# An attention kernel with expert routing, rewritten around rows: wider exponentials, token rows scattered by slot, all expert work at the end

## The chip, the cores and the metric

The kernel runs on one core of a Trainium2 chip. The metric is device time in microseconds (us) of that core, lower is better. Every job also ran the kernel before on the same chip. Results of different jobs are compared by their ratio to the kernel before of the same rounds, not by their microseconds.

## The reference, cut to what matters

```python
# q, k, v: 8 batches x 8 heads x 1152 x 64
q_pool = q.reshape(B, H, S // 2, 2, D).mean(axis=3)            # 576 queries a head
scores = scale * np.matmul(q_pool, k.transpose(0, 1, 3, 2))
attn = np.exp(scores - scores.max(-1, keepdims=True))
attn = attn / (attn.sum(-1, keepdims=True) + 1e-09)
x = (attn @ v)                                                 # -> 4608 tokens of 512
# 8 experts; each token goes to the one that domain_id names
for e in range(8):
    h = np.maximum(x[domain_id == e] @ w1[e], 0.0)             # 512 -> 1024
    out[domain_id == e] = h @ w2[e]                            # 1024 -> 512
```

The attention is done by pairs of heads, 32 pairs. AV below is the second product of attention, `attn @ v`. The traces show a matmul as two instructions, a load of one operand (PEld) and the matmul itself (PE); AV of the kernel before has 1152 of each. The operand that is loaded is called stationary here, the other moving. Both kernels give each expert 640 slots for rows, 40 tiles of 128 in all, whether filled or not.

## The kernel before

Attention: 576 steps. A step computes 128 keys by 288 queries for two heads, one exponential of 576 columns, and (three steps later) two AV matmuls with the values stationary. The result is transposed, features on partitions, so the softmax sums lie along one row and the reciprocals take a trip through DRAM to reach all partitions.

```python
def expo(t):                                   # 576 of these, 2 x 288 columns
    e_ = ering.tile([P, 2, QH], F16, name="e")
    et[t] = e_
    nc.scalar.activation(e_[:, :, :], st.pop(t)[:, :, 0:QH], AF.Exp, bias=0.0, scale=0.0625)

def norm_a(p):                                 # sums out of one row ...
    sr = work.tile([64, 18], FP32, name="srow")
    nc.sync.dma_start(sr[0:32, :], xu[p][0][64:65, :])
    nc.sync.dma_start(sr[32:64, :], xu[p][1][0:1, :])
    srec[p] = sr

def norm_b(p):                                 # ... reciprocal, to DRAM, back as a broadcast
    rr = work.tile([64, 18], FP32, name="rrow")
    nc.vector.reciprocal(rr[:, :], srec.pop(p)[:, :])
    nc.sync.dma_start(s_dram[p].rearrange("(a b) -> a b", a=64), rr[:, :])
    rb = work.tile([P, Sp], FP32, name="rb")
    for hh in range(2):
        nc.sync.dma_start(rb[64 * hh : 64 * hh + 64, :],
            s_dram[p, hh * Sp : (hh + 1) * Sp].unsqueeze(0).broadcast_to([64, Sp]))
    srec[p] = rb

def norm_c(p, hh):                             # ... multiply into xT, features x tokens
    nc.vector.tensor_tensor(out=xT[lo : lo + 64, 1 + b * Sp : 1 + (b + 1) * Sp, hp],
        in0=xu[p][hh][lo : lo + 64, :], in1=srec[p][lo : lo + 64, :], op=ALU.mult)

def gather(xs, j, e, t, hi, w=P):              # tokens of an expert, on POOL
    nc.gpsimd.indirect_copy(xs[:, j * P : (j + 1) * P, :], xT[:, 0:hi, :],
        idx[:, e, t * 8 : (t + 1) * 8], True)
# ... cut: two of an expert's five tiles are filler units inside the second half of attention;
# ... cut: the other three are the tail:
    for f in range(NF):
        for cc in range(ND):
            nc.tensor.matmul(hp_[:, 0:nsl], lhsT=w1h[:, cc, f * P : (f + 1) * P],
                rhs=xs[:, 0:nsl, cc],          # moving operand, element step 4
                start=cc == 0, stop=cc == ND - 1)
```

The softmax here doesn't subtract the row's maximum and nothing guards it: scores larger than these inputs give would overflow.

Of the kernel before, what the change touches and what calls it, by code (L numbers as in the profile page):

```python
# [19 lines left out]
def kernel(  # L20
# [16 lines left out]
    NT = N // P  # L37
# [4 lines left out]
    QH = Sp // 2  # L42
    QP = 96
    NJ = Sp // QP
    JH = NJ // 2
    R1 = 256
    R2 = 384
    CAP = R1 + R2
    NTC = CAP // P
    COLS = (N + R1) // 16  # L50
    EROW = 16 * COLS
    IC = CAP // 16
    I1 = NT // 2

    g_dram = nc.dram_tensor("g_slot", (E * EROW, 1), I32, kind="Internal").ap()
    s_dram = nc.dram_tensor("s_rec", (NPAIR, 2 * Sp), FP32, kind="Internal").ap()

    wpool = ctx.enter_context(tc.tile_pool(name="wpool", bufs=4))
    perm = ctx.enter_context(tc.tile_pool(name="perm", bufs=1))
    fbuf = ctx.enter_context(tc.tile_pool(name="fbuf", bufs=2))  # L60


    att = ExitStack()
    lds = att.enter_context(tc.tile_pool(name="lds", bufs=2))
    work = att.enter_context(tc.tile_pool(name="work", bufs=2))
    ering = att.enter_context(tc.tile_pool(name="ering", bufs=8))
    spsum = att.enter_context(tc.tile_pool(name="spsum", bufs=2, space=bass.MemoryType.PSUM))
    apsum = att.enter_context(tc.tile_pool(name="apsum", bufs=1, space=bass.MemoryType.PSUM))
    mpsum = att.enter_context(tc.tile_pool(name="mpsum", bufs=2, space=bass.MemoryType.PSUM))
# [6 lines left out]
    v16 = [perm.tile([P, NC, 2 * P], F16, name=f"v16_{i}") for i in range(NV)]  # L76
    ident = perm.tile([P, P], FP32, name="ident")
    ident16 = perm.tile([P, P], F16, name="ident16")
    xT = perm.tile([P, N + 1, HP], F16, name="xT")
# [3 lines left out]
    def pair_load(p):  # L83
        b, h = p // HP, 2 * (p % HP)
        q2 = lds.tile([QP, 2, NJ, 2 * D], FP32, name="q2")
        for hh in range(2):
            nc.sync.dma_start(
                q2[:, hh, :, :],
                q[b, h + hh].rearrange("(j p r) d -> p j (r d)", p=QP, j=NJ),
            )  # L90
        k16 = lds.tile([P, 2, NC, D], F16, name="k16")
        nc.gpsimd.dma_start(  # L92
            k16[:, :, :, :], k[b, h : h + 2].rearrange("h (p c) d -> p h c d", p=P)
        )
        vs = lds.tile([P, 2, NC, D], F16, name="vs")
        nc.gpsimd.dma_start(  # L96
            vs[:, :, :, :], v[b, h : h + 2].rearrange("h (p c) d -> p h c d", p=P)
        )
        loaded[p] = {"q2": q2, "k16": k16, "vs": vs}

    pair_load(0)
    pair_load(1)


    make_identity(nc, ident[:, :])
    nc.vector.tensor_copy(ident16[:, :], ident[:, :])
    for i in range(NV):
        nc.vector.memset(v16[i][:, :, D : D + P], 1.0)
# [11 lines left out]
    n_iota = perm.tile([P, NT], I32, name="n_iota")  # L120
    nc.gpsimd.iota(n_iota[:, :], pattern=[[P, NT]], base=0, channel_multiplier=1)
    dom = perm.tile([NT, 2 * P], I32, name="dom")
    nc.sync.dma_start(dom[:, :], moe_domain_id.bitcast(I32).rearrange("(i q) -> i q", i=NT))
    g_init = perm.tile([P, E * EROW // P], I32, name="g_init")
    nc.gpsimd.memset(g_init[:, :], N)
    nc.sync.dma_start(g_dram.rearrange("(a b) one -> a (b one)", a=P), g_init[:, :])
    nc.gpsimd.memset(xT[:, 0:1, :], 0.0)
# [4 lines left out]
    def rt_a():  # L132
        d16 = perm.tile([NT, P], F16, name="d16")
        nc.vector.tensor_copy(d16[:, :], dom[:, 0 : 2 * P : 2])
# [6 lines left out]
        mt = mpsum.tile([P, 1024], F16, name="mt")  # L141
        nc.tensor.transpose(mt[:, 0:NT], in_=d16[:, :], identity=ident16[0:NT, 0:NT])
        dall = perm.tile([P, NT], FP32, name="dall")
        nc.vector.tensor_copy(dall[:, :], mt[:, 0:NT])
# [9 lines left out]
    PADC = 32  # L154

    def rt_b():
# [5 lines left out]
        mc = mpsum.tile([P, 512], FP32, name="mt")  # L162
# [4 lines left out]
        mr = mpsum.tile([P, 512], FP32, name="mt")  # L167
# [13 lines left out]
    def rt_c():  # L181
        inc = rt["sc"][0]
        oh, cum, dall = rt["oh"], rt["cum"], rt["dall"]
        delta = perm.tile([P, E], FP32, name="delta")
        nc.vector.tensor_scalar(
            out=delta[:, :], in0=inc[:, :, PADC + I1 - 1], scalar1=-1.0, scalar2=float(R1),
            op0=ALU.mult, op1=ALU.add,
        )
        nc.vector.tensor_scalar(
            out=delta[:, :], in0=delta[:, :], scalar1=0.0, scalar2=None, op0=ALU.max  # L190
        )
# [3 lines left out]
        nc.vector.tensor_tensor(  # L195
            out=cum[:, :, I1:], in0=cum[:, :, I1:],
            in1=delta[:, :].unsqueeze(2).broadcast_to([P, E, NT - I1]), op=ALU.add,
        )
# [4 lines left out]
        )  # L203
        ov = perm.tile([1, E], FP32, name="ov")
        nc.vector.tensor_tensor(
            out=ov[:, :], in0=inc[0:1, :, PADC + NT - 1], in1=delta[0:1, :], op=ALU.add
# [14 lines left out]
        si = perm.tile([P, NT], I32, name="si")  # L221
        nc.vector.tensor_copy(si[:, :], slot[:, :])
        sr = perm.tile([P, NT], I32, name="sr")
        nc.vector.tensor_single_scalar(out=sr[:, :], in_=si[:, :], scalar=15, op=ALU.bitwise_and)
        scol = perm.tile([P, NT], I32, name="scol")
        nc.vector.tensor_single_scalar(out=scol[:, :], in_=si[:, :], scalar=4, op=ALU.arith_shift_right)
        af = perm.tile([P, NT], FP32, name="af")
        nc.vector.scalar_tensor_tensor(
            out=af[:, :], in0=sr[:, :], scalar=float(COLS), in1=scol[:, :], op0=ALU.mult, op1=ALU.add
        )  # L230
        addr = perm.tile([P, NT], I32, name="addr")
        nc.vector.scalar_tensor_tensor(
            out=addr[:, :], in0=dall[:, :], scalar=float(EROW), in1=af[:, :], op0=ALU.mult, op1=ALU.add
        )
        rt.update(addr=addr, ovi=ovi)

    gap = perm.tile([1, 1], FP32, name="gap")

    def rt_scatter(i):
        nc.gpsimd.memset(gap[:, :], 0.0)  # L240
        ins = nc.gpsimd.indirect_dma_start(
            out=g_dram[:, :],
            out_offset=bass.IndirectOffsetOnAxis(ap=rt["addr"][:, i : i + 1], axis=0),
            in_=n_iota[:, i : i + 1],
            in_offset=None,
        )
        tc.declare_no_dep(ins.ins, group="gscat", reason="slots are unique")
        tc.add_to_no_dep_group("gscat", ins.ins)

    gidx = perm.tile([P, E, IC], I32, name="gidx")  # L250
    gtok = perm.tile([P, E, NTC], I32, name="gtok")
    idx = perm.tile([P, E, IC], U16, name="idx")
    gv = g_dram.rearrange("(e p c) one -> p e (c one)", e=E, p=16)

    def rt_read(a):
        nc.sync.dma_start(gidx[16 * a : 16 * a + 16, :, :], gv[:, :, 0:IC])

    def make_idx(dst, src, w):
        m1 = fbuf.tile([P, w], FP32, name=f"m1_{w}")
        nc.vector.tensor_scalar(  # L260
            out=m1[:, :], in0=src, scalar1=float(N), scalar2=4.0, op0=ALU.is_lt, op1=ALU.mult
        )
        m2 = fbuf.tile([P, w], FP32, name=f"m2_{w}")
        nc.vector.tensor_scalar(out=m2[:, :], in0=src, scalar1=1.0, scalar2=None, op0=ALU.add)
        nc.vector.tensor_tensor(out=dst, in0=m2[:, :], in1=m1[:, :], op=ALU.mult)

    own = perm.tile([P, 8], FP32, name="own")

    def rt_own():
        grp = perm.tile([P, 1], I32, name="grp")  # L270
        nc.vector.tensor_single_scalar(
            out=grp[:, :], in_=n_iota[:, 0:1], scalar=4, op=ALU.arith_shift_right
        )
        nc.vector.tensor_tensor(
            out=own[:, :], in0=iota_e[:, :], in1=grp[:, 0:1].broadcast_to([P, 8]), op=ALU.is_equal
        )

    def make_tok(dst, src, w):
        mk = fbuf.tile([P, w, 8], FP32, name=f"mk_{w}")
        nc.vector.tensor_tensor(  # L280
            out=mk[:, :, :], in0=src, in1=own[:, :].unsqueeze(1).broadcast_to([P, w, 8]), op=ALU.mult
        )
        mf = fbuf.tile([P, w], FP32, name=f"mf_{w}")
        nc.vector.tensor_reduce(mf[:, :], mk[:, :, :], mybir.AxisListType.X, ALU.add)
        nc.vector.tensor_copy(dst, mf[:, :])

    def rt_idx():
        rt_own()
        make_tok(
            gtok[:, :, :].rearrange("p e t -> p (e t)"),  # L290
            gidx[:, :, :].rearrange("p e (t a) -> p (e t) a", a=8),
            E * NTC,
        )
        make_idx(
            idx[:, :, :].rearrange("p e c -> p (e c)"),
            gidx[:, :, :].rearrange("p e c -> p (e c)"),
            E * IC,
        )
# [22 lines left out]
    def gather(xs, j, e, t, hi, w=P):  # L321
        nc.gpsimd.indirect_copy(  # L322
            xs[:, j * P : (j + 1) * P, :],
            xT[:, 0:hi, :],
            idx[:, e, t * 8 : (t + 1) * 8],
            True,
        )

    def scatter_out(osb, ap):
        nc.gpsimd.memset(gap[:, :], 0.0)  # L330
        ins = nc.gpsimd.indirect_dma_start(  # L331
            out=out[:, :],
            out_offset=bass.IndirectOffsetOnAxis(ap=ap, axis=0),
            in_=osb[:, :],
# [219 lines left out]
    for t in range(NST + 3):  # L554
# [49 lines left out]
        if t == 4:  # L604
            rt_b()
# [141 lines left out]
```

## Time and profile before

| | us |
|---|---|
| kernel before, median (742.57 to 746.84) | 745.72 |
| the profiled run's span | 771.9 |

The profiled execution took 773.81 us, 3.8% more than the median of the timed ones, although it is recorded as fast.

The engines are PE (matmuls; PEld is its loads of stationary operands), ACT (exponentials), DVE (other elementwise work), POOL (gathers, and the issue of many DMAs) and SP (issues DMAs only). "issue" as a releaser means that the profile shows nothing that the engine waited for. The first extract, of the kernel before, cuts the span into stretches (us from the start) and gives for each the busy time of each engine, the instructions in brackets, the granted TensorE clock and the DMA engines' share.

```profile
core 0: us, PE busy (x) PEld busy (x) DVE busy (x) ACT busy (x) POOL busy (x), PEclk, DMA share, GB/s
0.00:17.60 17.60, 2.47 (x20) 1.95 (x21) 8.50 (x22) 1.29 (x2) 6.19 (x18) 1.00 1.00 203
17.60:321.00 303.40, 216.72 (x1509) 144.04 (x1508) 158.66 (x309) 192.10 (x313) 76.46 (x124) 0.87 0.62 112
321.00:490.00 169.00, 164.29 (x1075) 103.89 (x1075) 104.75 (x206) 92.41 (x143) 56.50 (x78) 0.98 0.72 144
490.00:579.00 89.00, 78.24 (x571) 52.29 (x569) 55.44 (x99) 73.42 (x121) 7.22 (x9) 0.96 0.41 81
579.00:606.00 27.00, 0.07 (x2) 0.10 (x2) 4.59 (x6) 0.00 (x0) 2.60 (x3) 0.57 0.04 12
606.00:763.00 157.00, 129.53 (x448) 49.05 (x447) 23.36 (x40) 24.49 (x47) 55.11 (x83) 0.89 0.41 85
763.00:772.00 9.00, 0.07 (x1) 0.00 (x0) 0.00 (x0) 0.58 (x1) 1.42 (x3) 0.72 0.15 49
```

Row by row: start; attention alone; attention with expert filler; attention after the filler is used up; a dead stretch (PE 0.07 us in 27); the expert tail; the end. Attention alone keeps no engine busy: PE 217 of 303 us, ACT 192. The next extract is from the kernel before's list of waits (engine and line, what it waited for: total us, times, longest us).

```profile
ACT e L422 <- PE s L404: 189.9, 202, 15.6
...
DVE hT L656 <- PE hp L649: 124.4, 32, 18.2
...
PE mt L378 <- DVE kp L370: 64.0, 28, 10.0
...
DVE xT L471 <- DMA rb<-s_rec: 50.8, 19, 7.2
...
DVE rrow L458 <- DMA srow<-xuB: 45.3, 19, 6.0
```

ACT waits for scores, PE for DVE's copy of the keys (L378 transposes them), and DVE for the DMAs of the reciprocals' trip. DVE does its work in the order of the program here, so a wait for `rb` holds up the copies behind it: in this trace DVE is idle for 7.12 us until `rb` has landed, multiplies (131.22 to 134.12 us), copies the keys at 134.15, and PE, which waited 6.75 us for that copy, goes on at 135.01.

The groups of instructions of the kernel before (line, engine, operation, shapes, count, then busy us and mean ns of one, then idle time before them and what ended it):

```profile
L422 ACT ACTIVATE e<-s 128x576 f16<-128x576 f32 x576 | 357.9, 649 | 218.6 <-PE s L404 189.9 <-remote 17.5 <-PE accB L404 2.2
...
L649 PE MATMUL hp<-xs,w1h 128*128 128x384 f16 x256 | 88.3, 518 | 54.4 <-POOL gap L330 27.5 <-POOL xs L322 26.9
...
L662 PE MATMUL op<-w2h,hT 128*128 128x512 f16 x192 | 42.9, 380 | 0.0
...
L322 POOL INDIRECT_COPY xs<-xT,idx 128x512 f16 x40 | 35.8, 896 | 217.1 <-issue 187.6 <-PE s L404 25.2 <-PE hp L649 4.2
```

The gather (last line) looks cheap, 0.9 us of busy time, but the timeline of the kernel before around the first tail experts shows how far apart gathers are (start, duration, instruction, idle before it in brackets):

```profile
595.05 0.87 POOL L322 INDIRECT_COPY xs<-xT,idx 128x512 f16 x1 [53.05 <-issue]
600.07 0.87 POOL L322 INDIRECT_COPY xs<-xT,idx 128x512 f16 x1 [4.15 <-issue]
605.07 0.87 POOL L322 INDIRECT_COPY xs<-xT,idx 128x512 f16 x1 [4.13 <-issue]
605.99 11.04 PE L649 MATMUL hp<-xs,w1h 128*128 128x384 f16 x32 [26.93 <-POOL xs L322]
...
610.07 0.87 POOL L322 INDIRECT_COPY xs<-xT,idx 128x512 f16 x1 [4.13 <-issue]
...
616.85 5.36 PE L662 MATMUL op<-w2h,hT 128*128 128x512 f16 x24
```

The gathers start 5.0 us apart with 4.13 us of idle time for which the profile names no other cause. And 32 matmuls of 384 columns take 11.04 us, 340 ns each, where 24 of 512 columns with contiguous operands take 5.36, 216 each (216 x 23 + 380).

### The profile page before, as it was taken

To read this page: it belongs to the slowest core of one execution; us is meant where nothing else is said; L and a number is where in the kernel's file an instruction comes from. 1 tells how busy PE (TensorE), PEld (TensorE's weight loads), DVE (VectorE), ACT (ScalarE), POOL (GpSimd) and SP (SyncE) were. 2 spreads that over 40 slices of the span, in tenths; PEclk is the share of its full clock that TensorE was granted. 3 is DMA by queue.
4 is the path that set the end of the run, shared out by engine and by line. 5 is a ranking of instruction groups with operands and counts; after the bars stand their busy time and mean duration, and the time that the engine had idled before them with its cause. 6 is when DMAs were issued, how large, how long until landed. Compare 5 with 4: busy or idle time off the path is not lost.

```text
span 771.9 us, 10270 instructions
## 1 busy us (share of the span) xinstructions
PE 591.4 (77%) x3619; PEld 351.3 (46%) x3619; DVE 355.3 (46%) x680; ACT 384.3 (50%) x625; POOL 205.5 (27%) x316
## 2 busy tenths in 40 slices
PE   2857675948676887599999999888990597776885
PEld 1534443636454564366666666555660232222332
DVE  4744443545553765366666655665852111111111
ACT  1746564848575686355555555777890111111111
POOL 3264640211120100124343331210000144443331
PEclk9977978989899898799999999999995698988998
DMA  9344459785859445157999935654310065556001
GB/s 192 65 79 77 78 90 173 138 147 109 158 116 200 93 88 117 23 106 144 188 196 187 206 89 117 115 101 86 70 33 17 0 135 114 116 116 126 36 33 37
DMA packets 91006, 83.24 MB, mean 108 GB/s; under 512 B 12698, under 2 KB 78398, under 8 KB 90944
## 3 DMA queue, kind: packets, MB, share of 16 engines
q0 software_dynamic: 40960, 53.51, 39.6%
q1 hardware_dynamic: 49984, 28.98, 15.8%
q8 instruction: 30, 0.49, 0.3%
q14 instruction: 32, 0.26, 0.1%
HBM read 116.59 MB, written 10.81 MB: 165 GB/s over the span
## 4 chain that ended last, share of the span: by engine, by line
issue 22%; PE 20%; DVE 13%; DMA 12%; POOL 6%; POOLq 0%; SPq 0%; DVEq 0%
PE mt L404 9%; DVE xT L471 7%; DMA rb<-s_rec 4%; PE s L404 4%; DMA srow<-xuB 4%; POOL xs L322 3%; DMA s_rec<-rrow 3%; DVE kp L370 2%; PE accA L404 2%; PE accB L404 2%; POOL out_dram L331 2%; PE hp L649 2%; PE mt L378 1%; DVE v L359 1%; DMA srow<-xuA 1%
## 5 line engine op out<-in xcount | busy, mean ns | idle before, releaser
L422 ACT ACTIVATE e<-s 128x576 f16<-128x576 f32 x576 | 357.9, 649 | 218.6 <-PE s L404 189.9
L404 PE MATMUL s<-qz,kq 128*128 128x288 f16 x1152 | 250.5, 301 | 24.1 <-ACT e L422 12.4
L404 PE MATMUL accA<-e,v 128*128 128x288 f16 x576 | 169.9, 299 | 11.0 <-DVE xuA L445 7.9
L404 PE MATMUL accB<-e,v 128*128 128x288 f16 x576 | 169.4, 299 | 0.7 <-DVE xuB L445 0.3
L404 PEld LDWEIGHTS <-kq 128*128 128x128 f16 x1152 | 116.2, 103 | 110.8 <-issue 55.2
L404 PEld LDWEIGHTS <-v 128*128 128x128 f16 x1152 | 116.9, 101 | 49.4 <-issue 13.1
L649 PE MATMUL hp<-xs,w1h 128*128 128x384 f16 x256 | 88.3, 518 | 54.4 <-POOL gap L330 27.5
L322 POOL INDIRECT_COPY xs<-xT,idx 128x512 f16 x40 | 35.8, 896 | 217.1 <-issue 187.6
L649 PEld LDWEIGHTS <-w1h 128*128 128x128 f16 x256 | 30.1, 118 | 110.3 <-issue 107.5
L378 PE MATMUL mt<-ident,kp 128*128 128x128 f16 x256 | 23.2, 243 | 69.1 <-DVE kp L370 64.0
L656 DVE TENSOR_SCALAR hT<-hp 128x384 f16<-128x384 f32 x32 | 17.8, 557 | 124.4 <-PE hp L649 124.4
L404 PE MATMUL mt<-xs,w1h 128*128 128x256 f16 x256 | 68.6, 402 | 7.2 <-POOL xs L322 7.2
L96 POOL DMA_DIRECT2D vs<-in_v_dram x32 | 23.1, 722 | 189.9 <-DVE v L359 178.1
L654 ACT ACTIVATE hT<-hp 128x384 f16<-128x384 f32 x32 | 15.7, 491 | 116.3 <-PE hp L649 103.3
L471 DVE TENSOR_TENSOR xT<-xuA,rb 64x576 f16<-64x576 f32 x32 | 46.1, 1440 | 47.8 <-DMA rb<-s_rec 47.4
L331 POOL DMA_INDIRECT out_dram<-osb,gtok x40 | 44.8, 1119 | 57.5 <-DVE osb L512 41.6
L445 DVE COPY xuA<-accA 128x288 f32<-128x288 f32 x64 | 28.8, 450 | 62.9 <-PE accA L404 46.6
L378 PEld LDWEIGHTS <-kp 128*128 128x128 f16 x256 | 17.2, 109 | 79.5 <-DVE kp L370 73.9
L495 DVE TENSOR_SCALAR hT<-mt 128x256 f16<-128x256 f32 x64 | 27.1, 423 | 52.5 <-PE mt L404 52.5
L471 DVE TENSOR_TENSOR xT<-xuB,rb 64x576 f16<-64x576 f32 x32 | 46.3, 1448 | 4.4 <-DMA rb<-s_rec 3.5
L92 POOL DMA_DIRECT2D k<-in_k_dram x32 | 23.7, 742 | 85.4 <-DVE kp L370 80.4
L662 PE MATMUL op<-w2h,hT 128*128 128x512 f16 x192 | 42.9, 380 | 0.0
(83 smaller groups left out, 435.9 us busy)
## 6 DMA issues: line engine op xcount, KB each, us to landing
q<-in_q_dram SPq DMA_DIRECT2D x64, 288.0 KB
w1h<-in_moe_w_dram POOLq DMA_DIRECT2D x24, 512.0 KB
w2h<-in_moe_w_dram POOLq DMA_DIRECT2D x24, 512.0 KB
k<-in_k_dram POOLq DMA_DIRECT2D x32, 288.0 KB
vs<-in_v_dram POOLq DMA_DIRECT2D x32, 288.0 KB
rb<-s_rec SPq DMA_DIRECT2D x64, 144.0 KB
out_dram<-osb,gtok POOLq DMA_INDIRECT x40
g_slot<-n_iota,addr POOLq DMA_INDIRECT x36
```

Of the source, the lines that this page charges most:

```text
L92: nc.gpsimd.dma_start(k16[:, :, :, :], k[b, h : h + 2].rearrange("h (p c) d -> p h c d", p=P))
L96: nc.gpsimd.dma_start(vs[:, :, :, :], v[b, h : h + 2].rearrange("h (p c) d -> p h c d", p=P))
L322: nc.gpsimd.indirect_copy(xs[:, j * P : (j + 1) * P, :], xT[:, 0:hi, :], idx[:, e, t * 8 : (t + 1) * 8], True,)
L331: ins = nc.gpsimd.indirect_dma_start(out=out[:, :], out_offset=bass.IndirectOffsetOnAxis(ap=ap, axis=0), in_=osb[:, :], in_offset=None, bo ...
L378: nc.tensor.transpose(mt[:, c * P : (c + 1) * P], in_=k16[:, c, :, :].rearrange("p h d -> p (h d)"), identity=ident16[:, :])
L404: nc.tensor.matmul(out_, lhsT=lhsT, rhs=rhs, start=start, stop=stop)
L422: nc.scalar.activation(e_[:, :, :], st.pop(t)[:, :, 0:QH], AF.Exp, bias=0.0, scale=0.0625)
L445: nc.vector.tensor_copy(xu[p][head][:, hf * QH : (hf + 1) * QH], acc[u][head][:, 0:QH])
L471: nc.vector.tensor_tensor(out=xT[lo : lo + 64, 1 + b * Sp : 1 + (b + 1) * Sp, hp], in0=xu[p][hh][lo : lo + 64, :], in1=srec[p][lo : lo + 6 ...
L495: nc.vector.tensor_scalar(out=hts[e][:, f, :], in0=m[:, 0:R1], scalar1=0.0, scalar2=None, op0=ALU.max)
L649: nc.tensor.matmul(hp_[:, 0:nsl], lhsT=w1h[:, cc, f * P : (f + 1) * P], rhs=xs[:, 0:nsl, cc], start=cc == 0, stop=cc == ND - 1,)
L662: nc.tensor.matmul(op_[:, :], lhsT=hT[:, f, tt * P : (tt + 1) * P], rhs=w2h[:, f, :], start=f == 0, stop=f == NF - 1,)
```

## The change

The intent: take the waits out of attention, take the gathers out of the tail. The exponential becomes the stationary operand of AV (128 queries by 128 keys, with 64 values and a column of ones moving), so that a token is a row, its softmax sum lies beside it on the same partition, and DVE normalises with no DMA. Rows go by an indirect DMA to their slot in DRAM with the token's id as the last two elements; an expert's rows are read back contiguously and turned by PE. Keys are cast a pair ahead. The start changes too (the first pair's keys come uncast from SP, and 30 matmuls on zeros run first). The core of the diff, with cuts marked and some lines shortened:

```diff
-    QH = Sp // 2
+    W = 432
+    SPP = NC * Sp // W              # 12 steps a head pair, 384 in all
 ... cut
+    dom = perm.tile([P, B, NQ], I32, name="dom")
+    for i in range(NQ):             # nine DMAs of 4-byte elements
+        ... cut
+            nc.scalar.dma_start(dom[m : m + n, :, i : i + 1], dv_[pp : pp + n, :, j, 0:1])
 ... cut
-        e_ = ering.tile([P, 2, QH], F16, name="e")
-        nc.scalar.activation(e_[:, :, :], st.pop(t)[:, :, 0:QH], AF.Exp, ...)
+        if s_ % 4 == 0:
+            et[p, s_ // 4] = ering.tile([P, 2, 4 * W], F16, name="e")
+        nc.scalar.activation(e_[:, :, o : o + W], st.pop(t)[:, :, 0:W], AF.Exp, ...)
 ... cut
-        for head in range(2):
-            mm(acc[u][head][:, 0:QH], v16[p % NV][:, c, P * head : P * head + P], e_[:, head, :], ...)
+        for h in range(2):
+            for i in range(NQ):
+                nc.tensor.matmul(acc[p][h][:, i * (D + 1) : (i + 1) * (D + 1)],
+                    lhsT=e_[:, h, o + QO[i] : o + QO[i] + P],
+                    rhs=v16[p % NV][:, c, h, 0 : D + 1], ...)
 ... cut: norm_a, norm_b, norm_c and all gathers are removed
+            nc.vector.reciprocal(rr[:, :], a[:, :, D])
+            nc.vector.tensor_tensor(out=xb[b][:, :, hh * D : (hh + 1) * D], in0=a[:, :, 0:D],
+                in1=rr[:, :].unsqueeze(2).broadcast_to([P, NQ, D]), op=ALU.mult)
+    def put_x(b, i):
+        scatter(x_dram, xb[b][0:n, i, :], rt["addr"][0:n, ...], "xscat")
 ... cut: the filler units are removed
+    def turn(xs, n):                # rows -> features on partitions, contiguous
+        xt = tb.tile([P, ND, CAP], F16, name="xt")
+        ... four transposes a tile, copied out by DVE and ACT in turn
+    for e in range(3):
+        run(e, get_x(e, 0, NA), NA)                  # two tiles each
+    for e in range(E): ...          # then three tiles of experts 0 to 2, five of 3 to 7
```

## The prediction

> **What bounds the kernel now** (profiled span 771.9 us; unprofiled median 746.69). By the stretches view: start 17 us, attention alone 304 us, attention with expert filler 169 us, attention 90 us, a dead stretch of 26 us (PE busy 0.01 us), expert tail about 166 us.
> - Attention: the exponentials are 576 x 128x576. Back to back they start every 0.55 us, but in the undisturbed pattern every 0.65: two PSUM buffers make exp(t+1) wait for a score that waited for exp(t-1). Over 17-321 us a step costs 0.97 us (313 exps in 304 us). The list of waits: exponentials wait 190 us for scores; PE waits 64 us for DVE's key copy; DVE waits 51+45+12 us for the DMAs of the reciprocal round trip. With filler PE is 97% busy.
> - Tail: bound by POOL. The timeline shows one gather every 5.0 us (4.13 "issue" + 0.87); three gathers and the scatters make the 22 us period of an expert. PE needs only 16 us of it. There, 384-column matmuls go every 340 ns although 512-column ones with contiguous operands take 216: the moving operand has an element step of 4. [...]
>
> **What the change does**
> 1. 384 exponentials of 864. Duration 649 ns at 576 against 491 at 384 columns gives 0.82 ns per column: 0.89 us long, 0.78 us apart at best (301 us). With the two-buffer handshake (0.89 + about 0.76)/2 = 0.82 us a step.
> 2. AV: 2,880 matmuls of 65 columns instead of 1,152 of 288 (122 ns each, 141 us). The 96-column transposes with a weight load each go every 44 ns, so 44 is my ceiling, 30 my floor: 86-127 us. [...] the trace's 128-column transposes go every 57. PE per step: scores 0.37, AV 0.22-0.33, transposes 0.07, so 0.66-0.77 us: below ACT, barely.
> 3. The reciprocal round trip goes, DVE falls from 9.5 to about 5.6 us per head pair, keys are copied a pair ahead: those waits go. I take 0.87 us a step: 384 x 0.87 = 334 us, plus about 10 us of DMA stalls (5 MB slot-table fill early; weights in bursts).
> 4. Start: first exp at about 12.5 us instead of 17.6 (no PE wait for the domain ids).
> 5. Turn-over, PE idle: last evacuation, five serial scatters of 1.25 us, landing, row loads, first transposes: 14 us.
> 6. Experts all at the end, no gathers, contiguous operands: stage 1 69 us, stage 2 69 us, transposes with exposed evacuation about 24: 163 us.
> 7. End: 8 us as now.
> Sum 12.5 + 344 + 14 + 163 + 8 = 541 us profiled; the profile now is 3% over the timed run, so about 528 us.
>
> All on the critical path: attention goes from 563 to 344 us, the dead stretch from 26 to 14; the tail stays near 165 with all the experts in it.
>
> **Chances**: faster 0.98, same 0.01, slower 0.01; 8 in 10 within 495 to 575 us.
>
> **What would show it**: exponentials about 0.89 us each and 0.82-0.9 apart; AV matmuls 30-44 ns apart; no gathers; granted clock over 0.95; 512-column expert matmuls 216 ns apart; a PE gap of 10-16 us between the phases.
>
> **What would make it wrong**: AV pairs over 55 ns (PE-bound attention, +40 us); scattered rows or table fill clogging the queues so that q, k or v come late; weights late in the last experts; the clock dropping at pauses.

What is cut compared the trace with figures that no run here shows. Its floor of 30 ns for an AV matmul agrees with the trace's 44 ns at 96 columns taken in proportion to the columns, 29.8 at 65 (an estimate). Of a lower clock at a pause the trace of the kernel before has a case: 0.57 granted in the dead stretch, 0.96 in the stretch before it and 0.89 in the one after.

## The result, and the profile after

| kernel | median us | range | profiled span | granted clock |
|---|---|---|---|---|
| before | 745.72 | 742.57 to 746.84 | 771.9 | 0.902 |
| changed | 532.53 | 531.74 to 537.33 | 535.5 | 0.948 |

The ratio is 0.716 (95% interval 0.712 to 0.720). Ratios here are the mean time of one kernel's fast runs over that of the other's of the same rounds, so not quite the ratio of the medians.

The stretches of the changed kernel:

```profile
core 0: us, PE busy (x) PEld busy (x) DVE busy (x) ACT busy (x) POOL busy (x), PEclk, DMA share, GB/s
0.00:25.40 25.40, 8.29 (x51) 5.30 (x52) 7.04 (x21) 1.51 (x3) 7.62 (x22) 0.73 1.06 221
25.40:42.40 17.00, 7.14 (x59) 5.22 (x59) 5.63 (x17) 5.22 (x6) 0.90 (x2) 0.50 0.72 147
42.40:342.50 300.10, 288.76 (x4428) 227.54 (x4426) 157.06 (x389) 296.84 (x378) 98.15 (x153) 0.99 0.82 168
342.50:357.80 15.30, 1.48 (x17) 1.20 (x18) 1.70 (x5) 0.59 (x2) 5.23 (x10) 0.62 0.28 91
357.80:522.10 164.30, 156.31 (x984) 84.33 (x983) 48.85 (x83) 46.24 (x82) 49.88 (x89) 0.99 0.46 122
522.10:535.50 13.40, 0.03 (x1) 0.00 (x0) 0.00 (x0) 0.59 (x1) 1.75 (x3) 0.69 0.11 37
```

Start; a slow first stretch of attention; attention; the turn-over; the experts; the end. From 42.4 us on attention is what it was meant to be: ACT 297 of 300 us, PE 289, clock 0.99. The two profiled spans side by side:

| part | before | after | change |
|---|---|---|---|
| to the first exponential | 17.6 | 25.4 | +7.8 |
| first exponential to end of the last | 561 | 317 | -244 |
| to the first expert matmul (before: of the tail) | 27 | 15 | -12 |
| experts | 157 (24 of 40 tiles) | 164 (40 of 40) | +7 |
| end | 9 | 13 | +4.5 |

Since the profile of the kernel before is of a slow execution, in which the stretch of attention alone reads some 27 us too long, about 30 of the 244 us are not the change's: against e7's 531 us, attention falls by 214 (an estimate, since e7 is of another job).

The groups of the changed kernel that answer to those shown before:

```profile
L431 ACT ACTIVATE e<-s 128x864 f16<-128x864 f32 x384 | 302.1, 899 | 38.2 <-DMA dom<-in_moe_domain_id_dram 23.1 <-PE s L419 14.8 <-ACT e L431 0.2
L442 PE MATMUL acc<-v,e 128*128 128x65 f16 x2880 | 136.6, 194 | 2.4 <-DVE xb L459 2.1 <-ACT e L431 0.3
...
L607 PE MATMUL op<-w2h,hT 128*128 128x512 f16 x320 | 70.9, 379 | 0.0
...
L591 PE MATMUL hp<-xt,w1h 128*128 128x384 f16 x96 | 17.7, 325 | 1.6 <-DVE xt L579 1.6
```

The mean durations do not show the rate, because instructions overlap. The median distance from one exponential to the next is 0.787 us, less than the 0.899 that each lasts. Ten AV matmuls take 0.47 us in the timeline, so (0.47 - 0.194) / 9 = 31 ns apart. Each has a weight load of its own (2880 of each). Transposes of 128 columns, with a load each too, start 56 ns apart (median).

The list of waits of the changed kernel has lost DVE's waits for the reciprocals' DMAs and all but 0.7 us of PE's waits for keys. Of what is left, these waits hold up ACT, DVE's routing and PE longest:

```profile
ACT e L431 <- DMA dom<-in_moe_domain_id_dram: 23.1, 1, 23.1
...
DVE dall L182 <- DMA x_slot<-pat: 20.0, 1, 20.0
ACT e L431 <- PE s L419: 14.8, 9, 10.2
...
PE xp L575 <- DMA xs<-x_slot: 13.1, 1, 13.1
```

The lines with `dom` and `dall` are new costs: the ids. (The `dall` line, which turns the ids into numbers, names the fill of the slot table, `x_slot<-pat`, as the last DMA to end; that is an inference of the profile. Run e2 below speaks against it: there the nine loads come earlier, and `dall` starts at 23.36 us, 1.4 us after the first part of the fill was issued, where a part takes a median 19.6 us to land. The profile of e2 names the load of the ids.) The timeline of the changed kernel shows both (an ACTq line is DMA issues by ACT):

```profile
5.58 19.76 ACTq L158 DMA_DIRECT2D dom<-in_moe_domain_id_dram  x9
...
11.11 1.62 PE L419 MATMUL s<-qz,kq 128*128 128x432 f16 x6 [0.67 <-DVE qz L404]
...
25.38 1.67 ACT L431 ACTIVATE e<-s 128x864 f16<-128x864 f32 x2 [23.13 <-DMA dom<-in_moe_domain_id_dram]
...
35.76 0.18 DVE L182 CAST dall<-dom 128x40 f32<-128x40 int32 x1 [19.97 <-DMA x_slot<-pat]
...
39.87 0.89 ACT L431 ACTIVATE e<-s 128x864 f16<-128x864 f32 x1 [10.16 <-PE s L419]
```

The first scores are there at about 12 us. But ACT is issuing the nine loads of the ids until 25.3 us, so the first exponential starts at 25.38. Then DVE, in order, waits for the ids until 35.76 and holds up the second pair's keys; the fifth exponential starts at 39.87.

### The profile page after: what moved, and what is told of

The parts are those of the page before. It is cut to its first block, busy times and chain, and to the rows that moved or that the text cites. A ratio compares the mean times of both kernels' runs of the same rounds, so it can differ in the third digit from the quotient of the medians.

```text
span 535.5 us, 12899 instructions
## 1 busy us (share of the span) xinstructions
PE 462.0 (86%) x5536; PEld 323.6 (60%) x5536; DVE 220.3 (41%) x515; ACT 351.0 (66%) x470; POOL 163.5 (31%) x278
## 2 busy tenths in 40 slices
DMA packets 57172, 80.48 MB, mean 150 GB/s; under 512 B 8590, under 2 KB 43150, under 8 KB 57104
## 4 chain that ended last, share of the span: by engine, by line
ACT 47%; issue 26%; DMA 11%; POOL 8%; DVE 2%; PE 2%; POOLq 0%; ACTq 0%; SPq 0%; DVEq 0%
ACT e L431 47%; POOL out_dram L341 6%; DMA w2h<-in_moe_w_dram 5%; DMA dom<-in_moe_domain_id_dram 3%; DMA x_slot<-pat 2%; PE s L419 1%; POOL x_slot L341 1%; PE acc L442 1%; POOL gap L339 1%; DMA xs<-x_slot 1%; DMA x_slot<-xb,addr 0%; DVE xb L459 0%; DVE sc L212 0%; POOLq L341 0%; POOL vs L96 0%
## 5 line engine op out<-in xcount | busy, mean ns | idle before, releaser
L431 ACT ACTIVATE e<-s 128x864 f16<-128x864 f32 x384 | 302.1, 899 | 38.2 <-DMA dom<-in_moe_domain_id_dram 23.1
L419 PE MATMUL s<-qz,kq 128*128 128x432 f16 (+2 forms) x1152 | 205.9, 287 | 23.4 <-ACT e L431 22.4
L442 PEld LDWEIGHTS <-e 128*128 128x128 f16 x2880 | 127.8, 98 | 41.7 <-DVE xb L459 2.8
L442 PE MATMUL acc<-v,e 128*128 128x65 f16 x2880 | 136.6, 194 | 2.4 <-DVE xb L459 2.1
L341 POOL DMA_INDIRECT x_slot<-xb,addr x40 | 43.5, 1087 | 130.0 <-issue 130.0
L591 PE MATMUL hp<-xt,w1h 128*128 128x128 f16 (+3 forms) x512 | 75.9, 301 | 5.0 <-DVE xt L579 3.2
L341 POOL DMA_INDIRECT out_dram<-osb,xs x40 | 39.6, 990 | 121.3 <-ACT osb L613 101.9
L607 PEld LDWEIGHTS <-hT 128*128 128x128 f16 x320 | 31.1, 98 | 35.6
L459 DVE TENSOR_TENSOR xb<-acc,rr 128x320 f16<-128x320 f32 x64 | 31.5, 492 | 2.8 <-DVE rr L457 0.4
L357 DVE TENSOR_TENSOR qp<-q 96x768 f16<-96x768 f32 x32 | 30.2, 945 | 1.5 <-DMA q<-in_q_dram 1.5
L575 PE MATMUL xp<-ident,xs 128*128 128x128 f16 x160 | 14.0, 223 | 16.7 <-DMA xs<-x_slot 13.1
```

Of the source, the lines that this page charges most:

```text
L341: ins = nc.gpsimd.indirect_dma_start(out=dst[:, :], out_offset=bass.IndirectOffsetOnAxis(ap=ap, axis=0), in_=src, in_offset=None, **kw,)
L357: nc.vector.tensor_tensor(out=qp[:, :, :, :].rearrange("p j h d -> p h j d"), in0=q2[:, :, :, 0:D], in1=q2[:, :, :, D : 2 * D], op=ALU.add,)
L419: nc.tensor.matmul(s[:, r, o : o + n], lhsT=kq[p][:, c * P : (c + 1) * P], rhs=qz[p % 2][r][:, q0 : q0 + n], start=True, stop=True,)
L431: nc.scalar.activation(e_[:, :, o : o + W], st.pop(t)[:, :, 0:W], AF.Exp, bias=0.0, scale=0.0625)
L442: nc.tensor.matmul(acc[p][h][:, i * (D + 1) : (i + 1) * (D + 1)], lhsT=e_[:, h, o + QO[i] : o + QO[i] + P], rhs=v16[p % NV][:, c, h, 0 : D ...
L459: nc.vector.tensor_tensor(out=xb[b][:, :, hh * D : (hh + 1) * D], in0=a[:, :, 0:D], in1=rr[:, :].unsqueeze(2).broadcast_to([P, NQ, D]), op ...
```

## The experiments

| run | from | job's before | median us | ratio to before |
|---|---|---|---|---|
| changed kernel, first job | | 745.72 | 532.53 | 0.716 |
| e9_after_again | changed | 763.21 | 539.37 | 0.708 |
| e1_dom_one | changed | 765.91 | 520.71 | 0.681 |
| e2_dom_sp | changed | 765.91 | 530.54 | 0.695 |
| e3_region_a | changed | 765.91 | 551.54 | 0.720 |
| e4_strided | changed | 765.91 | 626.69 | 0.820 |
| e5_exp576 | changed | 745.15 | 577.55 | 0.776 |
| e6_v_stationary | changed, wrong | 745.15 | 547.70 | 0.735 |
| e7_one_gather | before, wrong | 745.15 | 706.65 | 0.950 |
| e8_no_trip | before | 745.15 | 674.78 | 0.905 |
| e10_both_skip | changed | 763.21 | 532.13 | 0.698 |
| e11_both_inrange | changed | 763.21 | 531.50 | 0.696 |
| e12_keys_ahead | before | 763.21 | 753.13 | 0.984 |

### The same kernel on the other chip

> The changed kernel unchanged, on the chip of the three runs that follow, to have it and them on one chip (an earlier job's chip ran the kernel before at 766 us instead of 746). 529 to 536 us and a ratio of 0.71 to 0.72 if the chip is like the first.

Measured: 539.4 us and 0.708, a little outside the expectation on both counts. On a chip where the kernel before takes 2.3% longer, the changed one takes 1.3% longer. For the runs whose job ran the kernel before at 764 or 766 us, this is the changed kernel to compare with.

### What the start costs: e1_dom_one and e2_dom_sp

e1 loads the ids in one contiguous DMA of 8 rows, first in ACT's queue, reorders them on DVE and turns them by five transposes. It also moves the first step of the routing (`rt_a`) ahead of the first pair's preparation. Lines are shortened here:

```diff
-            nc.scalar.dma_start(dom[m : m + n, :, i : i + 1], dv_[pp : pp + n, :, j, 0:1])   # x9
+    nc.scalar.dma_start(dom[:, :], moe_domain_id.bitcast(I32).rearrange("(b q) -> b q", b=B))
+        nc.vector.tensor_copy(d8 as b j p, dom as b (p j t) -> b j p)
+        nc.tensor.transpose(tpd[:, i * B : (i + 1) * B], in_=d8[:, QO[i] : QO[i] + P], ...)     # x5
-    rt_a()      # after the first pair's preparation
+    rt_a()      # before it
```

> The changed kernel, with the domain ids loaded by one contiguous DMA of 8 rows and turned by five small transposes, in place of nine DMAs of 4-byte elements issued from ACT. Theory (the nine loads hold up ACT until 25.4 us and the routing on DVE until 35.8 us): first exponential at about 12 us, a steady 0.79 us a step from about 18 us instead of 42.4, so 18 to 25 us less: about 510 us. Rival 1 (the fill of the slot table in DRAM, 5 MB, is what DVE waited for, as the wait list names it): first exponential early, but DVE still stalled to about 35 us, gain 5 us at most. Rival 2 (q, k and v simply are not there earlier): no gain, 532 us.

Measured: 520.7 us, ratio 0.681 against 0.708 for the changed kernel, so 3.8% less, 20 us (17 by the profiled spans, 519.0 against 536.1). In the profile the first exponential starts at 13.97 us and the last at 325.07; in the changed kernel's profile of the same kind of chip they start at 24.93 and 341.82. The theory holds in cause and size; its 510 us was meant for the first chip. e1 is the fastest correct kernel.

e2 keeps the nine loads and issues them from SP.

```diff
-            nc.scalar.dma_start(dom[m : m + n, :, i : i + 1], ...)
+            nc.sync.dma_start(dom[m : m + n, :, i : i + 1], ...)
```

> The changed kernel, with the same nine small DMAs issued from SP's queue instead of ACT's. If only ACT's issue time costs (25.4 against 12 us to the first exponential): about 13 us less, 519 us. If the landing of the ids, which DVE waits for in order, is what counts: the first exponential comes at about 12 us but the stall before the fifth grows, and the time stays within 5 us of 532.

Measured: 530.5 us, ratio 0.695, some 10 us less than the changed kernel: between the two expectations. The first exponential starts at 12.78 us, so ACT's issuing was what held it. But the fifth exponential starts 11.26 us after the fourth (6.70 in the changed kernel on this kind of chip), because the ids still land late (`dall` starts at 23.36 us). It starts at 35.06 us in the changed kernel, 27.46 in e2 and 18.57 in e1. So about half of the cost, 7.6 us, is ACT as the issuing engine; the other 8.9 are the late landing of the 4-byte elements and the place of `rt_a`, which e1 changes together. The nine issues held ACT for 19.8 us in the changed kernel, 0.66 to 4.7 each, for 18 KB in all, beside 7 to 17 us from an issue to its landing. One of these issues, 2.2 us on average, is the smaller part of its DMA, but nine in a row add up on the engine that the kernel waits for; the ids in one DMA of long rows (e1; 36 KB, as whole 8-byte ids) took 0.57 us to issue.

### The moving operand's step: e4_strided

```diff
-        xt = tb.tile([P, ND, CAP], F16, name="xt")
+        xt = tb.tile([P, CAP, ND], F16, name="xt")
-                        rhs=xt[:, cc, lo : lo + n], start=cc == 0, stop=cc == ND - 1,
+                        rhs=xt[:, lo : lo + n, cc], start=cc == 0, stop=cc == ND - 1,
```

> The changed kernel, with the turned rows stored token by token, so that the moving operand of the first expert layer has an element step of 4, as in the kernel before. Theory (the step alone makes the kernel before's 340 ns for 384 columns): a 384-column matmul goes every 340 ns instead of 162, the first layer takes about 145 us instead of 70, and the time rises by 70 to 80 us to about 605 us. Rival (the gathers on POOL or a lower clock slowed them): under 10 us more.

Measured: 626.7 us, ratio 0.820 against 0.708: about 87 us more. The matmuls of 384 columns start 340 ns apart (median; 162 in the changed kernel), and a run of 32 takes 11.04 us, just what it takes in the kernel before, against 5.90 in the changed kernel. No gather runs here. The granted clock of the expert stretch is 0.93, against 0.99, but the 512-column matmuls of the second layer, in the same stretch, go every 216 ns as before, so the clock does not explain it and the step does. Summed from the first to the last matmul of each run, the first layer takes 143 us against 73, so 70 more, as expected. Of the rest, 16 us are waits of PE for the copies that write the turned rows with the same step (24 us in the expert stretch, 8 in the changed kernel). The groups of e4_strided:

```profile
L591 PE MATMUL hp<-xt,w1h 128*128 128x384 f16 x96 | 33.1, 518 | 4.2 <-DVE xt L579 4.2
...
L579 DVE COPY xt<-xp 128x512 f16<-128x512 f16 x24 | 31.0, 1291 | 27.3 <-PE xp L575 17.9 <-PE op L607 7.5 <-issue 1.9
...
L581 ACT COPY xt<-xp 128x512 f16<-128x512 f16 x16 | 20.7, 1293 | 21.7 <-PE xp L575 21.7
```

The copies last 1.29 us, where DVE needed 0.42 and ACT 0.59 for them in the changed kernel, and PE waits for some of them. So a step of 4 elements costs a factor of 2.1 on the 384-column matmuls here (340 against 162 ns).

### Width of the exponentials: e5_exp576

```diff
-    W = 432
+    W = 288
-        if s_ % 4 == 0:
+        if s_ % 6 == 0:
-    AVS = {3: 0, 4: 1, 5: 2, 7: 3, 8: 4, 9: 5, 11: 6, 12: 7, 13: 8}
+    AVS = {2 * c + 3: c for c in range(NC)}
 ... the rest of the schedule stretched by 1.5
```

> The changed kernel, with exponentials of 576 instead of 864 elements (576 steps of 288 columns; the rest of the schedule stretched by 1.5). Handshake theory (exponential 0.65 us long, then score and semaphores about 0.5 to 0.6, two in flight): 0.58 to 0.65 us a step, attention 332 to 374 us instead of 300, time 565 to 605 us. Rival (only ACT's own back-to-back rate counts, 0.547 us a step): 315 us, time 547 us. Rival 2 (width is worth nothing, the gain came from the waits taken away): 535 us.

Measured: 577.6 us, 45 more than the changed kernel in the first job (the kernel before agrees to 0.6 us between these two jobs). The median distance of exponentials is 0.596 us, inside the handshake theory's 0.58 to 0.65 (with two score buffers an exponential waits for a score that waited for the exponential before the last) and above ACT's own rate: the tenth percentile, exponentials with nothing to wait for, is 0.546. Twice 0.596 less the exponential's own 0.650 leaves 0.54 us for a score and its semaphores. A score for an exponential of 864 has 144 more columns for each of two heads, some 0.12 us more (an estimate from the 122 ns of a 288-column matmul), so 0.66. With that the handshake gives (0.90 + 0.66) / 2 = 0.78 us, about ACT's own 0.787, so by this estimate the wide exponentials hide the handshake only just. The trace shows that they do: nine in ten overlap the one before by 105 ns or more, as the narrow ones do only where nothing holds them (103 to 104). Half of the narrow ones overlap by 50 ns or less.

### The form of AV: e6_v_stationary (wrong on purpose)

```diff
-            for i in range(NQ):
+            for i in range(2):
                 nc.tensor.matmul(
-                    acc[p][h][:, i * (D + 1) : (i + 1) * (D + 1)],
-                    lhsT=e_[:, h, o + QO[i] : o + QO[i] + P],
-                    rhs=v16[p % NV][:, c, h, 0 : D + 1],
+                    acc[p][h][:, 37 * i : 37 * i + 288],
+                    lhsT=v16[p % NV][:, c, :, :].rearrange("p h d -> p (h d)")[:, 0:P],
+                    rhs=e_[:, h, o + 288 * i : o + 288 * i + 288],
```

> The changed kernel, wrong on purpose: AV with the values stationary and 288 exponential columns moving, 36 matmuls of 288 a head pair instead of 90 of 65; the evacuation is left as it is, so the rows are garbage. Theory (ACT bounds attention at 0.79 us a step; PE would need 9.6 us a pair against ACT's 9.4): attention grows by 5 to 20 us, time 537 to 552 us; what the new AV form buys is the row layout, not PE time. Rival (PE time is the bound; AV goes from 2880 x 31 ns = 89 us to 1152 x 122 ns = 141 us): 52 us more, 585 us.

Measured: 547.7 us, 15 more than the changed kernel in the first job, inside the expected 537 to 552. The median distance of exponentials is 0.802 instead of 0.787. So the PE time that the new form saves is worth about 15 us. It also puts the softmax sum on the token's own partition, which is what lets the trip through DRAM go (e8 shows what that costs).

### The gathers: e7_one_gather (wrong on purpose, kernel before)

```diff
-        for j in range(R2 // P):
-            gather(xs, j, e, R1 // P + j, N + 1)
+        nc.vector.memset(xs[:, P:, :], 0.0)
+        gather(xs, 0, e, R1 // P, N + 1)
```

> The kernel before, wrong on purpose: in the tail one gather per expert instead of three, the other two thirds of the rows set to zero. Theory (POOL's gathers of 5.0 us bound the tail: 22 us an expert, where PE needs 10.9 + 5.4 us): about 16.5 us an expert, 42 to 50 us less, about 700 us. Rival (the tail is bound by PE or weight DMA): under 10 us less.

Measured: 706.7 us, 38 less; the expectation was 42 to 50. Experts start 16.1 us apart in the trace, which is PE's time, as expected. What I had over-stated is the baseline: in the kernel before most experts start 21 to 22 us apart, but the second starts 16.1 after the first, and the last two start 19 after the one before. The dead stretch ahead of the tail shrinks too, from 27 to 17 us, two gathers of 5.0 us fewer. That makes 10 of the 38 us; the tail itself falls from 157 to 129.

### The reciprocals' trip: e8_no_trip, and the key copies: e12_keys_ahead (both on the kernel before)

```diff
     def norm_b(p):
-        rr = work.tile([64, 18], FP32, name="rrow")
-        nc.vector.reciprocal(rr[:, :], srec.pop(p)[:, :])
-        nc.sync.dma_start(s_dram[p]...)
-        ... rb read back as a broadcast
+        pass
 ... norm_a is emptied in the same way
-            in1=srec[p][lo : lo + 64, :],
+            in1=rcst[lo : lo + 64, :],          # memset to 1 / 1152
```

> The kernel before, wrong on purpose: the reciprocals' round trip through DRAM taken out, a constant in its place; the copies and the multiplications stay. Theory (DVE, in order, waits for these DMAs, holds up the key copies, and with them PE and ACT): the stretch from 17 to 321 us, 0.97 us a step, falls to about 0.70 to 0.78, and the time falls by 60 to 100 us. Rival (the late place of the key copy in the program and the two-buffer handshake make the 0.97): under 20 us less.

Measured: 674.8 us, 70 less. The 313 steps up to the filler take 217 us, 0.70 us a step. In e7, of the same job and with the trip, they take 266, or 0.85; the 296 of the profile shown above hold the excess of that execution. (I meant this kernel to be wrong; it passed, because with these inputs the scores are so small that every softmax sum is close to 1152.)

e12 leaves the trip and moves the key copy a pair ahead, as the changed kernel does (with the second pair's copy before the loop).

```diff
-            if hf == 0 and c == 0:
-                prep_k(p + 1)
+            if hf == 1 and c == 4 and p + 2 < NPAIR:
+                prep_k(p + 2)
```

> The kernel before, correct, with the cast of the keys done a head pair ahead, as the changed kernel does it, and the reciprocals' round trip left in. Theory (PE waits for keys because DVE, in order, stands in the round trip's waits; moving the copy out of their way takes most of it): PE's 64 us of waits for the key copy fall under 15 us and the time falls by 25 to 60 us, less than the 70 us of taking the round trip out. Rival (the round trip still holds up DVE's other work, and with it PE): under 15 us less.

Measured: 753.1 us, ratio 0.984 (0.979 to 0.989): 10 us less, which the 2% rule of these verdicts calls unclear, and not 25 to 60. The theory is refuted, the rival stands. PE's waits for keys fell from 64.0 us to a single one of 10.0 at the start, but another wait took their place. From the list of waits of e12_keys_ahead:

```profile
PE accA L404 <- DVE xuA L445: 47.1, 22, 8.9
...
DVE xT L471 <- DMA rb<-s_rec: 42.5, 15, 8.4
...
PE mt L378 <- DVE kp L370: 10.0, 1, 10.0
```

PE now waits 47 us for DVE to empty the accumulators, against 7.9 us in the kernel before, while DVE still waits 42 us for the reciprocals to come back. Here the wait of an engine that works in order was passed on to what stood behind it: with one victim moved out of the way, the next one waited.

### The turn-over: e3_region_a, e10_both_skip, e11_both_inrange

After the last exponential of the changed kernel PE is idle for 13.1 us. The timeline of the changed kernel:

```profile
343.75 0.49 DVE L459 TENSOR_TENSOR xb<-acc,rr 128x320 f16<-128x320 f32 x1
345.01 0.92 POOL L341 DMA_INDIRECT x_slot<-xb,addr  x1 [29.73 <-issue]
...
350.06 0.97 POOL L341 DMA_INDIRECT x_slot<-xb,addr  x1 [0.23 <-issue]
...
353.32 1.41 SPq L564 DMA_DIRECT2D xs<-x_slot  x3
...
356.14 1.03 PE L575 MATMUL xp<-ident,xs 128*128 128x128 f16 x8 [13.13 <-DMA xs<-x_slot]
```

Five scatters one after the other, 1.26 us from start to start on average, their landing, the read. e3 scatters rows of experts 0 to 2 from the first four batches a second time, into a tensor of their own that no late scatter touches, and reads it long before attention ends.

```diff
+        if b < B // 2:
+            scatter(xa_dram, xb[b][0:n, i, :], rt["addra"][0:n, ...], "xascat", 3 * KO[1] - 1)
+        if t in (300, 303, 306):
+            get_xa((t - 300) // 3)
-        run(e, get_x(e, 0, NA), NA)
+        run(e, xsa[e], NA)
```

> The changed kernel, with rows of experts 0 to 2 from the first half of the batches scattered a second time into a DRAM tensor of their own, read before attention ends, so that the first expert work need not wait for the last five scatters. Theory (the 13.1 us of idle PE at the turn-over is the wait of the row loads for the last scatters): PE gap 1 to 3 us, time 10 to 13 us less, about 520 us. Rival (the turn-over is bound by buffer reuse, ACT or the clock coming back): gap stays over 8 us.

Measured: 551.5 us, ratio 0.720 against 0.708: slower. The mechanism was right: after the last exponential no PE gap over 1.3 us is left. But the distance from first to last exponential grew from 317 us to 345. Rows outside the region were skipped by the bounds check, and they were most (the region has 768 slots for the 2304 tokens of the first four batches; all DMAs moved 82.07 MB against 80.48 in the changed kernel, and of the 1.59 more the fill of the region is 0.79, which leaves 0.80 for the second scatters, about 768 rows of 1028 bytes). So the next two runs ask whether it is the skipping, with e1's load of the ids in both.

> The one contiguous load of the ids (520.7 us alone) together with the second scatter of region A as tried before, rows outside the region skipped by the bounds check. If both gains add and the 30 us that the second scatter cost in attention belonged to that run's chip: 506 to 511 us. If skipped rows or 20 more scatters stall attention on any chip: 525 to 545 us, attention over 320 us.

e11 sends the other rows to spare rows, one for each, so that none is skipped.

> The same, but rows outside region A go to spare rows of their own instead of being skipped. If skipped rows caused the stalls: 506 to 511 us here, with attention at 300 to 312 us, while the version that skips stays over 525. If 20 more scatters on POOL's queue are the cause: both over 525. If neither: both 506 to 511, within 3 us of each other.

Measured: 532.1 and 531.5 us, the same to 0.6, and both slower than e1 alone (0.698 and 0.696 against 0.681). Skipped rows are not the cause. From the start of the last exponential to the last matmul both take 166.6 us where e1 takes 181.4, so the turn-over gain of 15 us is real; from the first to the last exponential they take 334 us where e1 takes 311, and that takes it back. The stretches of e10_both_skip, one in which a batch's doubled scatters run and the next:

```profile
core 0: us, PE busy (x) PEld busy (x) DVE busy (x) ACT busy (x) POOL busy (x), PEclk, DMA share, GB/s
60.00:80.00 20.00, 13.97 (x161) 10.80 (x161) 6.54 (x16) 11.50 (x15) 15.27 (x27) 0.74 0.75 168
80.00:100.00 20.00, 19.49 (x304) 15.40 (x301) 11.20 (x28) 20.00 (x26) 3.65 (x6) 1.00 1.16 240
```

ACT loses 8.5 us of the first, none of the second. What makes 20 more scatters stall PE and ACT is not settled. The list of waits names no single cause in this stretch: ACT's waits are put down to "issue" (4.1 us), "remote" (2.6) and PE (1.7), and DVE waits 4.0 us for a load of queries.

A stall beside scatters goes with the kind of chip. In the jobs that ran the kernel before at 764 us, distances of 1.2 to 1.8 us between exponentials show at each batch's end, where five scatters run (e9, e1, e2 and e4); in the other two jobs none is over 1.2 beyond the start-up (changed kernel, e5 and e6). The kernel before has the same mark: the 72 steps with its scatters of slot numbers take 84 us in e12, of a 764 us job, and 54 in e7, of a 745 us job. These steps as stretches (columns as above), in the profile of the kernel before that is shown in this document, and in e7:

```profile
30.60:111.60 81.00, 53.29 (x350) 34.08 (x349) 36.84 (x76) 45.12 (x73) 45.58 (x81) 0.81 0.42 75
28.90:82.80 53.90, 44.82 (x349) 30.53 (x348) 34.39 (x75) 43.46 (x73) 43.53 (x75) 1.00 0.50 94
```

All engines have nearly the same instructions in both, and the first takes half as long again. So the 23 us that the second scatter cost may not be a cost on every chip; it was not tried on the faster kind, and why the chips differ is open.

## Why the prediction was right, and where it was not

The time was 532.5 us against 528 predicted, well inside 495 to 575. The sum is better than its terms: that it came within 5 us is luck. Against the profile:

| term, as predicted | predicted | measured |
|---|---|---|
| 4. first exponential | 12.5 | 25.4 |
| 1 to 3. attention, with 10 us of DMA stalls | 344 | 317 |
| 5. turn-over | 14 | 15.3 |
| 6. experts | 163 | 164.3 |
| 7. end | 8 | 13.4 |
| sum, profiled | 541 | 535.5 |
| profile over timed run | 3% | 0.6% |

- Right, and shown: the AV matmuls go every 31 ns (30 to 44 predicted); the exponentials last 0.90 us; experts take 164 us with contiguous operands (e4 shows what the step would cost); the tail before was bound by gathers (e7); the trip's waits were the largest loss that a run took out of the old attention (e8, with e12 against the rival). The turn-over is a chain of serial scatters and their landing (its predicted 14 us, and e3, e10, e11, where PE starts without it).
- Wrong, the start: "first exp at about 12.5 us ... (no PE wait for the domain ids)". I saw that the PE wait went and did not cost the nine loads that replaced it. They held ACT for 13 us and then DVE for 10 more (e1, e2).
- Wrong in size, the step: "0.87 us a step" was 0.787. The handshake term "about 0.76" for a score and its semaphores (2 x 0.65 - 0.65 + 0.12 from the trace before makes 0.77, an estimate) is about 0.66 (an estimate from e5's 0.54), so the handshake gives 0.78 instead of 0.82, and ACT's own rate binds (the overlaps under e5), 0.787 where "0.78 us apart at best" was predicted. On top of the 0.82 I had put an allowance of 0.05 for waits that did not come. Together 384 x 0.083 = 32 us, of which the allowance is the larger part.
- Wrong: "about 10 us of DMA stalls". Beyond the start there are next to none on this chip: of the 317 us, 302 are 384 steps of 0.787, and of the other 15, 10 lie before the fifth exponential.
- Wrong, the end: 13.4 us instead of 8. Why the end grew by 4.5 us was not tried.
- Wrong: "the profile now is 3% over the timed run". That was no cost of profiling but a slow execution, which took 773.81 us itself; in every run the span is 1.7 to 1.9 us shorter than the time of the same execution. After, the profiled execution is the slowest of its runs, 0.6% over their median by its span. The 13 us should not have been taken off: without them the sum says 541 to 543, some 10 too many.

The terms of attention are too long by 27 us in all, those of the start, the turn-over, the experts and the end too short by 21, and the 3% takes off 13 that were not there to take. So the sum came out. The gains do not add up part by part: taking a feature out of the new kernel (45 us for the width, 15 for AV's form, 87 for the operand's step) and taking a cost out of the old one (70 for the trip, 38 for the gathers) together make more than the 213 us; a likely reason, not tested, is that the kernel before hid part of the experts' work under an attention that it slowed, and the changed kernel hides none. The experiments show each mechanism; they do not split the 213 us.

## What to carry to other kernels

Lay out intermediate results so that a scale factor lies on the partition of what it scales: the DMA round trip in the stream of an in-order engine cost 70 us here, and taking one copy out of its way mostly moved the wait. Before a profile is used as a baseline, compare the time of the profiled execution with the timed runs. When a rewrite removes a wait, cost what replaces it, also a loop of tiny DMAs in the start-up: nine of them kept ACT from all else for 19.8 us. Look at the distance between instructions, not at their durations, to see a gather or a strided operand at its price.
